# A fused linear-attention and mixer kernel: batch 1's front divided anew between VectorE and ScalarE, and its steps placed anew among batch 0's matmuls

## The chip, the cores and the metric

The kernel runs on one core of a Trainium2 chip. Its time is device microseconds (us) of that core, as the median of several executions. TensorE (PE) multiplies into PSUM, VectorE (DVE) and ScalarE (ACT) move and change data and empty PSUM, GpSimd (POOL) and SyncE (SP) issue transfers, and all engines work through instruction queues of their own in order, held together by semaphores.

## The reference

There are 8 batches, 8 heads, 576 rows and 64 columns per head. Linear attention gives x, and a mixer works on it, first across rows (tokens) and then across channels.

```python
def phi(x): return np.where(x > 0, x, np.exp(x) - 1.0) + 1.0
q_p, k_p = phi(q), phi(k)
kv  = np.einsum('bhsd,bhse->bhde', k_p, v);  z = np.sum(k_p, axis=2)
num = np.einsum('bhsd,bhde->bhse', q_p, kv)
den = np.einsum('bhsd,bhd->bhs', q_p, z)[..., None] + 1e-06
x = (num / den)                               # as (8, 576, 512)
h = np.maximum(x.transpose(0, 2, 1) @ w_tok1, 0.0) @ w_tok2      # 576 -> 256 -> 576
u = x + h.transpose(0, 2, 1)
out = u + np.maximum(u @ w_ch1, 0.0) @ w_ch2                     # 512 -> 1536 -> 512
```

## The kernel before, in words

Rows are laid out as 9 slots of 64. A batch has four full tiles of 128 rows (`r` = 0 to 3) and one half tile (`r = R = 4`, 64 rows). The half tiles of the two batches of a pair are put together in one tile `ut` and are taken through the channel mixer once for both.

The steps of a batch, by the names that the change and the prediction use:

- `phi_exp`, `phi_add`, `phi_end` (L125, L131, L139 and L140): phi of half of q's or k's heads, as exp on ScalarE, then x + 1, a minimum and a maximum on VectorE. `vcast` (L151) casts v.
- `qtr` (L180, copied by L187): q transposed by PE, in batch 1 only; later batches do it with a DMA (`qtr_dma`).
- `kv` (L169): k^T v for all heads, with a column of ones for z, then two copies to `kvbd` (L175).
- `nd` (L210, then L219, L221, L222): numerator and denominator of x for two row tiles and half the heads (`g`), six times a batch. VectorE adds the epsilon, takes the reciprocal and multiplies.
- `mm1` (L248, ReLU on ScalarE L251), `mm2` (L261): the token mixer's two matmuls. `mm2` leaves u = x + h. Batch 1 has it as `mm2_half`, by halves of the columns (L297, L300): row tiles 0 and 1 add x by a matmul with the identity and are copied by ScalarE (L303), row tiles 2 and 3 are added by VectorE (L305). The last rows of batch 0 are made by `mm2_first_tail` (L458), those of batch 1 by `mm2(1, [R])`, those of later pairs by `mm2_tails` (L282, L286).
- `utr` (L316): u transposed by PE for batch 1, by pairs of column tiles; `utr_tail` (L481) transposes `ut`.
- `mm3` (L503, ReLU L510 or, on VectorE, L507), `mm3_tail` (L517), `mm4` (L529) and `mm4_end` (L546): the channel mixer, its sum with u and the transfer of the result.

The order is written out by hand. `run` takes a list of large steps (`big`: `mm3` and `mm4` of one batch) and a list of fillers with the number of the large step that each follows; these make the next batch's front. For batch 0, `m4_0(kc)` goes through `mm4` of all four row tiles with one piece of the contraction at a time, and its four accumulators (`held`) take all four banks of `ps_big`. The front of batch 1 therefore works in `ps_sm`, a pool of two buffers of two PSUM banks each, taken in turn: a step that wants a buffer waits till the one two places before it has been emptied. After the last `m4_0` came, in a row, output sums, `mm2_half`, `utr` and `mm2(1, [R])`, and only then `mm3` of batch 1.

```python
    work = ctx.enter_context(tc.tile_pool(name="work", bufs=2))
    ps_big = ctx.enter_context(tc.tile_pool(name="ps_big", bufs=4, space=bass.MemoryType.PSUM))
    ps_sm = ctx.enter_context(tc.tile_pool(name="ps_sm", bufs=2, space=bass.MemoryType.PSUM))
```

The transfers of batch 1's k, q and v and of the second piece of `w_ch2` are gated on earlier transfers; batch 2's q waits for that second piece.

Of the kernel before, what the change touches and what calls it, by code (L numbers as in the profile page):

```python
# [9 lines left out]
FP32 = mybir.dt.float32  # L10
# [8 lines left out]
def kernel(  # L19
# [26 lines left out]
    R = 4  # L46
# [115 lines left out]
    def kv(n, cs):  # L162
        b = n % 2
        ps = ps_sm.tile([128, 2, 512], FP32, name="kv_ps", tag="sm")[:, :, 0:2 * D1].rearrange(
            "p a (c e) -> p a c e", c=2)
        for c in cs:
            for t in range(T):
                for a, i in QUARTERS:
                    nc.tensor.matmul(out=ps[half[i], a, c], lhsT=kp[half[a], c, t, i],  # L169
                                     rhs=vs[half[a], 2 * c + i, t],  # L170
                                     start=(t == 0), stop=(t == T - 1))
        cs = slice(cs[0], cs[-1] + 1)
        for i in range(2):
            at = slice(i * D1, (i + 1) * D1)
            nc.scalar.copy(out=kvbd[b][half[i], cs, :, at].transpose([0, 2, 1, 3]),  # L175
                           in_=ps[half[i], :, cs])

    def qtr_mm(c, ts, tp):
        for s_, t in enumerate(ts):
# [48 lines left out]
    def nd(n, g, rs):  # L228
        nd_mm(n, g, rs)
        nd_end(n, g, rs)  # L230

    ALL = slice(0, DM)
    COLS = [slice(0, DM // 2), slice(DM // 2, DM)]

# [7 lines left out]
    def mm1(n):  # L242
        b = n % 2
        ps = ps_sm.tile([128, NT, DM], FP32, name="a_ps", tag="sm")
        for mt in range(NT):
            ms = slice(128 * mt, 128 * mt + 128)
            for r in range(R1):
                nc.tensor.matmul(out=ps[:, mt], lhsT=w1t[:, b, ms] if r == R else w1[:, r, ms],  # L248
                                 rhs=x[b][:, r, :], start=(r == 0), stop=(r == R))
        for mt in range(NT):  # L250
            nc.scalar.activation(out=ar[b][:, mt, :], in_=ps[:, mt], func=AF.Relu)  # L251

    def mm2(n, rs, add=False):

        b = n % 2
        m = len(rs)
        ps = bank().rearrange("p (a d) -> p a d", a=1) if n == 1 else ps_sm.tile(
            [128, 2, DM], FP32, name="h_ps", tag="sm")
        for i, r in enumerate(rs):
            for kt in range(NT):  # L260
                nc.tensor.matmul(out=ps[:, i], lhsT=w2v(kt, r, b),  # L261
# [2 lines left out]
            if add:  # L264
                nc.tensor.matmul(out=ps[:, i], lhsT=identity, rhs=x[b][:, r, :], start=False,
                                 stop=True)
        if rs[0] == R:
            h = half[b]
            nc.vector.tensor_tensor(out=ut[n // 2 % 2][h], in0=ps[h, 0], in1=x[b][h, R], op=ALU.add)
        elif add:  # L270
            nc.scalar.copy(out=u[b][:, rs[0]:rs[0] + m], in_=ps[:, 0:m])
        else:
            nc.vector.tensor_tensor(out=u[b][:, rs[0]:rs[0] + m], in0=ps[:, 0:m],  # L273
                                    in1=x[b][:, rs[0]:rs[0] + m], op=ALU.add)
# [10 lines left out]
            h = half[b]  # L285
            nc.vector.tensor_tensor(out=ut[p % 2][h], in0=ps[h], in1=x[b][h, R], op=ALU.add)  # L286

    def mm2_half(n, c):
        b = n % 2
        cs = COLS[c]  # L290
        for rs in ([0, 1], [2, 3]):
            ps = ps_sm.tile([128, 2, 512], FP32, name="h_ps", tag="sm")[:, 0].rearrange(
                "p (r c) -> p r c", r=2)
            add = rs[0] == 0
            for i, r in enumerate(rs):
                if add:
                    nc.tensor.matmul(out=ps[:, i], lhsT=identity, rhs=x[b][:, r, cs],  # L297
                                     start=True, stop=False)
                for kt in range(NT):
                    nc.tensor.matmul(out=ps[:, i], lhsT=w2v(kt, r), rhs=ar[b][:, kt, cs],  # L300
                                     start=(kt == 0 and not add), stop=(kt == NT - 1))
            if add:
                nc.scalar.copy(out=u[b][:, 0:2, cs], in_=ps)  # L303
            else:
                nc.vector.tensor_tensor(out=u[b][:, 2:4, cs], in0=ps, in1=x[b][:, 2:4, cs],  # L305
                                        op=ALU.add)

    def utr(n, js):
        b = n % 2
        for jp in js:  # L310
            tp = ps_sm.tile([128, 2, 8, 128], BF16, name="tp", tag="sm")[:, 0].rearrange(
                "p (j r) c -> p j r c", j=2)
            for i in range(2):
                j = 2 * jp + i
                for r in range(R):
                    nc.tensor.transpose(out=tp[:, i, r, :],  # L316
                                        in_=u[b][:, r, 128 * j:128 * j + 128], identity=identity)
            dst = uT[b][:, :, 2 * jp:2 * jp + 2].transpose([0, 2, 1, 3])
            if jp == 0:
                nc.vector.tensor_copy(out=dst, in_=tp)  # L320
            else:
                nc.scalar.copy(out=dst, in_=tp)

# [119 lines left out]
    def mm2_first(c, rs):  # L445
        cs = COLS[c]
        ps = bank().rearrange("p (r c) -> p r c", r=2)
        for i, r in enumerate(rs):
            for kt in range(NT):
# [1 line left out]
                                 start=(kt == 0), stop=(kt == NT - 1))  # L451
        nc.vector.tensor_tensor(out=u[0][:, rs[0]:rs[0] + 2, cs], in0=ps,
                                in1=x[0][:, rs[0]:rs[0] + 2, cs], op=ALU.add)

    def mm2_first_tail():
        ps = sm_tile()[:, 0]
        for kt in range(NT):
            nc.tensor.matmul(out=ps[half[0]], lhsT=w2p[:, D * (T * kt + 2 * R):][:, 0:D],  # L458
                             rhs=ar[0][:, kt],
                             start=(kt == 0), stop=(kt == NT - 1))  # L460
        nc.vector.tensor_tensor(out=ut[0][half[0]], in0=ps[half[0]], in1=x[0][half[0], R],
                                op=ALU.add)

    def utr_first(js, put):
        tp = ps_sm.tile([128, 2, 8, 128], BF16, name="tp", tag="sm")[:, 0].rearrange(
# [234 lines left out]
    def steps(n):  # L700

        out_ = [("kv", lambda: kv(n, range(2)))]
        if n == 1:
            puts = [nc.scalar.copy, nc.vector.tensor_copy if n == 1 else nc.scalar.copy]
            out_ += [(f"qt{c}", lambda c=c: qtr(n, c, puts[c])) for c in range(2)]
        for i, rs in enumerate(([0, 1], [2, 3], [4])):
            for g in range(2):
                out_.append((f"nd{i}{g}", lambda g=g, rs=rs: nd(n, g, rs)))
        out_.append(("mm1", lambda: mm1(n)))
        if n > 1:  # L710
            out_ += [("mm2a", lambda: mm2(n, [0, 1])), ("mm2b", lambda: mm2(n, [2, 3]))]
            if n % 2:
                out_.append(("mm2t", lambda: mm2_tails(n // 2)))
            out_ += [("uta", lambda: utr_dma(n, [0, 1])), ("utb", lambda: utr_dma(n, [2, 3]))]
            if n % 2:
                out_.append(("utt", lambda: utr_tail_dma(n // 2)))
        return out_

    def run(bigs, fill):
        for i, big in enumerate(bigs):  # L720
            big()
            for s, fn in fill:
                if s == i:
                    fn()
        for s, fn in fill:
            assert s < len(bigs)

    m3 = lambda n, k0=0: [lambda mc=mc: mm3(n, mc) for mc in range(k0, NCH)]
    m3t = [lambda i=i: mm3_tail(i) for i in range(3)]
# [1 line left out]
                        for t in ts for i in range(3)]  # L731


    def m4_0(kc):
        for t in range(R):
            mm4(0, t, [kc], wait=True)

    big = [lambda mc=mc: mm3(0, mc, range(2, 4)) for mc in range(3)] + \
        [lambda mc=mc: mm3(0, mc, dve=mc in (3, 6, 9)) for mc in range(3, NCH)] + \
        [lambda kc=kc: m4_0(kc) for kc in range(NCH)]  # L740
    at0 = {"qt0": 12, "qt1": 14, "vc": 13, "kv": 14, "nd00": 15, "nd01": 16, "nd10": 17,
           "nd11": 18, "nd20": 19, "nd21": 20, "mm1": 21}
    fill = [(2, mm2_first_tail)]
    for ex, ad, en, nm, c in ((2, 2, 3, "k", 0), (5, 5, 6, "k", 1), (8, 8, 9, "q", 0),
                              (11, 11, 12, "q", 1)):
        fill += [(ex, lambda nm=nm, c=c: phi_exp(nm, 1, 2 * c, 2)),
                 (ad, lambda nm=nm, c=c: phi_add(nm, 1, 2 * c, 2)),
                 (en, lambda nm=nm, c=c: phi_end(nm, 1, 2 * c, 2))]
    late = [("vc", lambda: vcast(1, 0)), ("vc", lambda: vcast(1, 1, nc.vector.tensor_copy))]
    fill += [(21, lambda g=g: phi("q", 2, g)) for g in range(2)]  # L750
    fill += [(22, lambda: qtr_dma(2)), (22, lambda: load_all(3, "qkv"))]
    first = steps(1)
    for nm, fn in first[1:2] + late + first[2:3] + first[0:1] + first[3:]:
        fill += [(at0[nm], fn)]
    fill += [(23, fn) for fn in (
        lambda: mm4_end(0, 0), lambda: mm4_end(0, 1), lambda: mm2_half(1, 0),
        lambda: mm4_end(0, 2), lambda: mm2_half(1, 1), lambda: utr(1, [0]),
        lambda: mm2(1, [R]), lambda: utr(1, [1]), lambda: mm4_end(0, 3))]
    run(big, sorted(fill, key=lambda e: e[0]))


    for mc in range(3):
        mm3(1, mc, range(0, 2))
    utr_tail(0)
    big = [lambda mc=mc: mm3(1, mc, range(2, 4)) for mc in range(3)] + [lambda mc=mc: mm3(1, mc, dve=mc in (5, 8)) for mc in range(3, NCH)] + m3t + m4(0, [4, 5, 6, 7, 8])
    at1 = {"kv": 8, "nd00": 10, "nd01": 11, "nd10": 12, "nd11": 13, "nd20": 14, "nd21": 15,
           "mm1": 17, "mm2a": 18, "mm2b": 19, "mm2t": 21, "uta": 18, "utb": 19}
    fill = [(s, lambda g=g: phi("k", 2, g)) for g, s in ((0, 0), (1, 2))]
    fill += [(4, lambda: vcast(2, 0)), (5, lambda: vcast(2, 1, nc.vector.tensor_copy))]
    fill += [(at1[nm], fn) for nm, fn in steps(2)]  # L770
# [59 lines left out]
```

## Time and profile before

| what | value |
|---|---|
| median of 3 runs | 263.5 us (263.29 to 263.62) |
| profiled execution | 263.5 us, of which the span is 261.7 us |
| PE, VectorE, ScalarE, POOL busy | 252.9, 158.6, 130.8, 35.7 us |
| granted TensorE clock | 1.000 |
| batch 1's front, `nd` to the first `mm3` of batch 1 | 38.9 to 53.5 us |

The span runs from the first to the last instruction. An operation's row gives line, engine, operation, what it writes and reads, shape and count. Matmuls are pipelined, so one is shown longer than the time till the next one starts.

### The profile page before, as it was taken

How to read it: one execution, taken by the hardware profiler on the slowest of the kernel's cores; microseconds unless marked ns; L12 is line 12 of the kernel's file. 1: busy time of each engine (PE TensorE's matmuls, PEld its weight loads, DVE VectorE, ACT ScalarE, POOL GpSimd, SP SyncE). 2: the span in 40 equal slices, each digit the busy share in tenths (PEclk: the TensorE clock that was granted, in tenths of full speed). 3: DMA queues.
4: the chain of work that ended last, by engine and by line, in shares of the span. 5: the costliest groups of instructions: out<-in, count | busy, mean ns of one | idle time of the engine just before them, and what ended most of it. 6: DMA issues, size and time to landing. Idle time of an engine off the chain costs nothing.

```text
span 261.7 us, 5138 instructions
## 1 busy us (share of the span) xinstructions
PE 252.9 (97%) x2102; PEld 132.5 (51%) x2102; DVE 158.6 (61%) x313; ACT 130.8 (50%) x202; POOL 35.7 (14%) x58
## 2 busy tenths in 40 slices
PE   7699999999999999999999999999999999999994
PEld 3484455554744554455554554455564554444642
DVE  5765969966739686948674377939674263420122
ACT  4664873378374468336780468235780453026300
POOL 9760220110001300030001300030001300000000
PEclk9999999999999999999999999999999999999999
DMA  7999999899407994799999970860075500730043
GB/s 251 256 204 273 382 187 364 251 189 379 181 8 141 203 369 196 153 234 380 407 313 212 361 297 1 172 161 21 3 143 109 123 3 2 154 105 0 3 102 98
DMA packets 50087, 48.34 MB, mean 185 GB/s; under 512 B 30288, under 2 KB 35536, under 8 KB 50064
## 3 DMA queue, kind: packets, MB, share of 16 engines
q1 hardware_dynamic: 41904, 35.53, 46.1%
q0 software_dynamic: 7440, 11.44, 21.0%
q10 hardware_dynamic: 720, 1.05, 1.2%
q8 instruction: 16, 0.26, 0.4%
q14 instruction: 7, 0.06, 0.1%
HBM read 35.85 MB, written 9.44 MB: 173 GB/s over the span
## 4 chain that ended last, share of the span: by engine, by line
PE 91%; DMA 3%; ACT 2%; POOL 1%; issue 1%; DVE 1%; ACTq 0%; POOLq 0%
PE h_ps L529 33%; PE c_ps L503 32%; PE a_ps L248 6%; PE c_ps L517 4%; PE h_ps L261 4%; PE nd_ps L210 3%; DMA cr<-in_v_dram 3%; PE kv_ps L169 2%; PE h_ps L566 1%; PE bank L440 1%; POOL qT L610 1%; PE bank L378 1%; PE h_ps L282 1%; PE bank L405 1%; ACT u L303 0%
## 5 line engine op out<-in xcount | busy, mean ns | idle before, releaser
L503 PE MATMUL c_ps<-uT,wc 128*128 128x512 bf16 x384 | 91.5, 379 | 0.0
L510 ACT ACTIVATE cr<-c_ps 128x512 bf16<-128x512 f32 x91 | 53.4, 599 | 75.6 <-PE c_ps L503 75.4
L529 PE MATMUL h_ps<-wc,cr 128*128 128x512 bf16 x372 | 84.9, 379 | 0.0
L529 PEld LDWEIGHTS <-cr 128*128 128x128 bf16 x372 | 35.7, 98 | 41.6 <-issue 1.2
L503 PEld LDWEIGHTS <-wc 128*128 128x128 bf16 x384 | 35.8, 98 | 36.6 <-issue 1.2
L551 POOL DMA_DIRECT2D out_dram<-o_sb x24 | 14.5, 606 | 150.8 <-DVE o_sb L546 150.6
L546 DVE TENSOR_TENSOR o_sb<-h_ps,u 128x512 f32<-128x512 f32 x31 | 21.0, 687 | 21.0 <-PE h_ps L529 21.0
L222 DVE TENSOR_TENSOR x<-nd_ps,den 128x512 bf16<-128x512 f32 (+1 forms) x42 | 25.3, 602 | 1.5
L139 DVE TENSOR_SCALAR e<-e 128x1152 bf16<-128x1152 bf16 x30 | 14.0, 468 | 15.6 <-ACT e L125 15.5
L125 ACT ACTIVATE e<-q_raw 128x1152 bf16<-128x1152 f32 x16 | 18.5, 1160 | 6.2 <-DMA q_raw<-in_q_dram 6.2
L273 DVE TENSOR_TENSOR u<-h_ps,x 128x1024 bf16<-128x1024 f32 x12 | 14.3, 1218 | 10.1 <-PE h_ps L261 10.1
L125 ACT ACTIVATE e<-k_raw 128x1152 bf16<-128x1152 f32 x16 | 18.7, 1169 | 2.4 <-DMA k_raw<-in_k_dram 2.3
L219 DVE TENSOR_SCALAR den<-nd_ps 128x8 f32<-128x8 f32 (+1 forms) x42 | 6.8, 163 | 17.9 <-PE nd_ps L210 17.2
L210 PEld LDWEIGHTS <-qT 128*128 128x128 bf16 x140 | 11.4, 98 | 9.3 <-issue 0.2
L210 PE MATMUL nd_ps<-kvbd,qT 128*128 128x130 bf16 x140 | 15.1, 223 | 0.0
L248 PE MATMUL a_ps<-x,w 128*128 128x512 bf16 x56 | 14.4, 379 | 0.0
L556 DVE TENSOR_TENSOR o_sb<-h_ps,ut 128x512 f32<-128x512 f32 x4 | 2.8, 689 | 18.7 <-PE h_ps L529 18.7
L151 ACT CAST vs<-v_raw 128x1152 bf16<-128x1152 f32 x12 | 13.9, 1160 | 0.0
L251 ACT ACTIVATE ar<-a_ps 128x512 bf16<-128x512 f32 x14 | 7.6, 595 | 11.0 <-PE a_ps L248 11.0
L261 PE MATMUL h_ps<-ar,w2p 128*128 128x512 bf16 x48 | 12.5, 379 | 0.1
L140 DVE TENSOR_TENSOR qp<-e,y 128x1152 bf16<-128x1152 bf16 x16 | 12.1, 758 | 0.6
L131 DVE TENSOR_SCALAR y<-q_raw 128x1152 bf16<-128x1152 f32 x16 | 12.1, 757 | 0.3
(111 smaller groups left out, 221.7 us busy)
## 6 DMA issues: line engine op xcount, KB each, us to landing
k_raw<-in_k_dram SPq DMA_DIRECT2D x16, 576.0 KB, 9.4
q_raw<-in_q_dram SPq DMA_DIRECT2D x16, 576.0 KB, 7.7
v_raw<-in_v_dram SPq DMA_DIRECT2D x14, 576.0 KB, 11.1
out_dram<-o_sb POOLq DMA_DIRECT2D x24, 256.0 KB, 4.7
wc<-in_moe_w_ch_dram POOLq DMA_DIRECT2D x8, 384.0 KB, 9.7
out_dram<-o_sb SPq DMA_DIRECT2D x9, 128.0 KB, 2.3
out_dram<-o_sb ACTq DMA_DIRECT2D x7, 128.0 KB, 2.6
out_dram<-o_sb POOLq DMA_DIRECT2D x6, 128.0 KB, 5.4
```

The costliest lines, as they stand in the source:

```text
L125: nc.scalar.activation(out=e, in_=f, func=AF.Exp)
L139: nc.vector.tensor_scalar(out=e, in0=e, scalar1=1.0, scalar2=None, op0=ALU.min)
L210: nc.tensor.matmul(out=o[:, a], lhsT=qT[b][:, t0:t0 + 128], rhs=kvbd[b][:, c, a], start=True, stop=True)
L222: nc.vector.tensor_tensor(out=x[b][:, rs[0]:rs[0] + m, HG * D * g:HG * D * (g + 1)].rearrange("p r (h d) -> p r h d", h=HG), in0=v_[:, :, ...
L248: nc.tensor.matmul(out=ps[:, mt], lhsT=w1t[:, b, ms] if r == R else w1[:, r, ms], rhs=x[b][:, r, :], start=(r == 0), stop=(r == R))
L261: nc.tensor.matmul(out=ps[:, i], lhsT=w2v(kt, r, b), rhs=ar[b][:, kt, :], start=(kt == 0), stop=(kt == NT - 1 and not add))
L273: nc.vector.tensor_tensor(out=u[b][:, rs[0]:rs[0] + m], in0=ps[:, 0:m], in1=x[b][:, rs[0]:rs[0] + m], op=ALU.add)
L503: nc.tensor.matmul(out=ps, lhsT=wc1[:, kj, 128 * mc:128 * mc + 128], rhs=uT[b][:, :, kj], start=(kj == 0), stop=(kj == NDM - 1))
L510: nc.scalar.activation(out=cr[b][:, mc, :], in_=ps, func=AF.Relu)
L529: nc.tensor.matmul(out=ps, lhsT=crt[:, kc, :] if t == 8 else cr[b][:, kc, 128 * r:128 * r + 128], rhs=wc2[:, kc, :], start=(kc == 0), stop ...
L546: nc.vector.tensor_tensor(out=o, in0=ps, in1=u[b][:, r, :], op=ALU.add)
L551: (nc.scalar if last and e else put).dma_start(out=outv[2 * p + b, :, 2 * r0 + e:2 * r0 + e + 2 * m - 1:2], in_=live["o"][half[e], 0:m])
```

## The change

Batch 1's front is built from other pieces and placed elsewhere.

- `nd_two` takes the place of `nd` for batch 1. VectorE scales two of four heads and ScalarE the other two, as activations of 64 columns with the reciprocal as scale. The half tile of both halves of the heads is one such step, so there are five in place of six.
- The second of the two copies to `kvbd`, and the ReLU of the second half of `mm1`, go to VectorE in batch 1.
- `mm1` stands at 19.5 in place of 21. `mm2` goes by full rows (`mm2_half` is gone), and `utr` transposes two row tiles at a time, both copied by ScalarE. Both stand among the `m4_0` steps and no longer behind them.
- `m4_0` is divided: by two row tiles for each piece of the contraction, and by single row tiles for the last two pieces.
- `mm2_first_tail` and `mm2(1, [R])` are replaced by `mm2_tails(0)`, which takes the last rows of batches 0 and 1 together.
- phi of batch 2's q, its transposing transfer and the loads of batch 3 stand at 19.5 and 20.5 in place of 21 and 22.

```diff
@@ kv
-            nc.scalar.copy(out=kvbd[b][half[i], cs, :, at].transpose([0, 2, 1, 3]),
-                           in_=ps[half[i], :, cs])
+            copy = nc.vector.tensor_copy if n == 1 and i else nc.scalar.copy
+            copy(out=kvbd[b][half[i], cs, :, at].transpose([0, 2, 1, 3]), in_=ps[half[i], :, cs])
@@ new
+    def nd_two(rs, gs):
+        b = 1
+        ps = ps_sm.tile([128, 2, 512], FP32, name="nd_ps", tag="sm")
+        at = [(r, g) for r in rs for g in gs]
+        for s_, (r, g) in enumerate(at):
+            o = ps[:, s_, 0:4 * D1].rearrange("p (i a e) -> p a i e", i=2, a=2)
+            for a in range(2):
+                t0 = D * (T * (2 * a + g) + 2 * r - (b if r == R else 0))
+                nc.tensor.matmul(out=o[:, a], lhsT=qT[b][:, t0:t0 + 128], rhs=kvbd[b][:, g, a],
+                                 start=True, stop=True)
+        v_ = ps[:, :, 0:HG * D1].rearrange("p s (h e) -> p s h e", h=HG)
+        den = work.tile([128, 2, HG], FP32, name="den", tag="den")
+        nc.vector.tensor_scalar(out=den, in0=v_[:, :, :, D:D1].rearrange("p s h o -> p s (h o)"),
+                                scalar1=EPS, scalar2=None, op0=ALU.add)
+        nc.vector.reciprocal(out=den, in_=den)
+        xs = x[b].rearrange("p r (g h d) -> p r g h d", g=2, h=HG)
+        dst = xs[:, R] if len(gs) == 2 else xs[:, rs[0]:rs[0] + 2, gs[0]]
+        nc.vector.tensor_tensor(out=dst[:, :, 0:2], in0=v_[:, :, 0:2, 0:D],
+                                in1=den[:, :, 0:2, None].to_broadcast([128, 2, 2, D]), op=ALU.mult)
+        for s_, (r, g) in enumerate(at):
+            for h in range(2, HG):
+                nc.scalar.activation(out=xs[:, r, g, h], in_=v_[:, s_, h, 0:D], func=AF.Copy,
+                                     scale=den[:, s_, h:h + 1])
@@ mm1
-            nc.scalar.activation(out=ar[b][:, mt, :], in_=ps[:, mt], func=AF.Relu)
+            if n == 1 and mt:
+                nc.vector.tensor_scalar(out=ar[b][:, mt, :], in0=ps[:, mt], scalar1=0.0,
+                                        scalar2=None, op0=ALU.max)
+            else:
+                nc.scalar.activation(out=ar[b][:, mt, :], in_=ps[:, mt], func=AF.Relu)
@@ utr
+    def utr(n, rs):
+        b = n % 2
+        tp = ps_sm.tile([128, 2, 8, 128], BF16, name="tp", tag="sm")[:, 0].rearrange(
+            "p (r j) c -> p r j c", r=2)
+        for i, r in enumerate(rs):
+            for j in range(NDM):
+                nc.tensor.transpose(out=tp[:, i, j, :],
+                                    in_=u[b][:, r, 128 * j:128 * j + 128], identity=identity)
+        nc.scalar.copy(out=uT[b][:, rs[0]:rs[0] + 2], in_=tp)
@@ the order
-        [lambda kc=kc: m4_0(kc) for kc in range(NCH)]
-    at0 = {"qt0": 12, "qt1": 14, "vc": 13, "kv": 14, "nd00": 15, "nd01": 16, "nd10": 17,
-           "nd11": 18, "nd20": 19, "nd21": 20, "mm1": 21}
-    fill = [(2, mm2_first_tail)]
...
-    fill += [(23, fn) for fn in (
-        lambda: mm4_end(0, 0), lambda: mm4_end(0, 1), lambda: mm2_half(1, 0),
-        lambda: mm4_end(0, 2), lambda: mm2_half(1, 1), lambda: utr(1, [0]),
-        lambda: mm2(1, [R]), lambda: utr(1, [1]), lambda: mm4_end(0, 3))]
+    at = list(range(NCH))
+    for kc in range(NCH - 2):
+        for h in range(2):
+            big.append(lambda kc=kc, h=h: m4_0([kc], [2 * h, 2 * h + 1]))
+            at.append(NCH + kc + h / 2)
+    for t in range(R):
+        big.append(lambda t=t: m4_0([NCH - 2, NCH - 1], [t]))
+        at.append(2 * NCH - 2 + t)
...
+    fill += [(12.5, lambda: qtr(1, 0)), (13.5, lambda: vcast(1, 0)),
+             (13.5, lambda: vcast(1, 1, nc.vector.tensor_copy)),
+             (14.5, lambda: qtr(1, 1, nc.vector.tensor_copy)), (14.5, lambda: kv(1, range(2))),
+             (15.5, lambda: nd_two([0, 1], [0])), (15.5, lambda: nd_two([0, 1], [1])),
+             (17, lambda: nd_two([2, 3], [0])), (18, lambda: nd_two([2, 3], [1])),
+             (18.5, lambda: nd_two([R], [0, 1])), (19.5, lambda: phi("q", 2, 0)),
+             (19.5, lambda: mm1(1)), (19.5, lambda: phi("q", 2, 1)),
+             (20.5, lambda: mm2(1, [0, 1], add=True)), (20.5, lambda: mm2(1, [2, 3])),
+             (20.5, lambda: qtr_dma(2)), (20.5, lambda: load_all(3, "qkv")),
+             (21.5, lambda: mm2_tails(0)), (21.5, lambda: utr(1, [0, 1])),
+             (22, lambda: mm4_end(0, 0)), (22, lambda: utr(1, [2, 3])),
+             (23, lambda: mm4_end(0, 1)), (24, lambda: utr_tail(0)), (24, lambda: mm4_end(0, 2)),
+             (25, lambda: mm4_end(0, 3))]
+    run(big, fill, at)
```

The three first `mm3` of batch 1, which stood in two parts around `utr_tail(0)`, are whole again and follow it.

More of the change, by code (lines that the diff above doesn't have):

```diff
@@ L256, in mm2 @@
         m = len(rs)
-        ps = bank().rearrange("p (a d) -> p a d", a=1) if n == 1 else ps_sm.tile(
-            [128, 2, DM], FP32, name="h_ps", tag="sm")
+        ps = ps_sm.tile([128, 2, DM], FP32, name="h_ps", tag="sm")
         for i, r in enumerate(rs):
@@ L266, in mm2 @@
                                  stop=True)
[L267 to L270, printed above, removed]
+        if add:
             nc.scalar.copy(out=u[b][:, rs[0]:rs[0] + m], in_=ps[:, 0:m])
@@ L286, in mm2_tails @@
             nc.vector.tensor_tensor(out=ut[p % 2][h], in0=ps[h], in1=x[b][h, R], op=ALU.add)
-    def mm2_half(n, c):
+    def utr(n, rs):
         b = n % 2
[L290 to L322, printed above, removed]
+        tp = ps_sm.tile([128, 2, 8, 128], BF16, name="tp", tag="sm")[:, 0].rearrange(
[5 more added lines that the diff above has]
+        nc.scalar.copy(out=uT[b][:, rs[0]:rs[0] + 2], in_=tp)
     COLS = [slice(0, DM // 2), slice(DM // 2, DM)]
@@ L453, in mm2_first @@
                                 in1=x[0][:, rs[0]:rs[0] + 2, cs], op=ALU.add)
[L455 to L462, printed above, removed]
     def utr_first(js, put):
@@ L702, in steps @@
         out_ = [("kv", lambda: kv(n, range(2)))]
-        if n == 1:
-            puts = [nc.scalar.copy, nc.vector.tensor_copy if n == 1 else nc.scalar.copy]
-            out_ += [(f"qt{c}", lambda c=c: qtr(n, c, puts[c])) for c in range(2)]
         for i, rs in enumerate(([0, 1], [2, 3], [4])):
@@ L709, in steps, with run @@
         out_.append(("mm1", lambda: mm1(n)))
[L710 to L716, printed above, removed]
-        return out_
-    def run(bigs, fill):
-        for i, big in enumerate(bigs):
+        out_ += [("mm2a", lambda: mm2(n, [0, 1])), ("mm2b", lambda: mm2(n, [2, 3]))]
+        if n % 2:
+            out_.append(("mm2t", lambda: mm2_tails(n // 2)))
+        out_ += [("uta", lambda: utr_dma(n, [0, 1])), ("utb", lambda: utr_dma(n, [2, 3]))]
+        if n % 2:
+            out_.append(("utt", lambda: utr_tail_dma(n // 2)))
+        return out_
+    def run(bigs, fill, at=None):
+        at = range(len(bigs)) if at is None else at
+        for i, big in zip(at, bigs):
             big()
@@ L725, in run @@
         for s, fn in fill:
-            assert s < len(bigs)
+            assert s in at
     m3 = lambda n, k0=0: [lambda mc=mc: mm3(n, mc) for mc in range(k0, NCH)]
@@ L731, with m4_0 @@
                         for t in ts for i in range(3)]
-    def m4_0(kc):
-        for t in range(R):
-            mm4(0, t, [kc], wait=True)
+    def m4_0(kcs, ts):
+        for t in ts:
+            mm4(0, t, kcs, wait=True)
     big = [lambda mc=mc: mm3(0, mc, range(2, 4)) for mc in range(3)] + \
-        [lambda mc=mc: mm3(0, mc, dve=mc in (3, 6, 9)) for mc in range(3, NCH)] + \
-        [lambda kc=kc: m4_0(kc) for kc in range(NCH)]
-    at0 = {"qt0": 12, "qt1": 14, "vc": 13, "kv": 14, "nd00": 15, "nd01": 16, "nd10": 17,
-           "nd11": 18, "nd20": 19, "nd21": 20, "mm1": 21}
-    fill = [(2, mm2_first_tail)]
+        [lambda mc=mc: mm3(0, mc, dve=mc in (3, 6, 9)) for mc in range(3, NCH)]
+    at = list(range(NCH))
[6 more added lines that the diff above has]
+        at.append(2 * NCH - 2 + t)
+    fill = []
     for ex, ad, en, nm, c in ((2, 2, 3, "k", 0), (5, 5, 6, "k", 1), (8, 8, 9, "q", 0),
-                              (11, 11, 12, "q", 1)):
+                              (11, 11, 12.5, "q", 1)):
         fill += [(ex, lambda nm=nm, c=c: phi_exp(nm, 1, 2 * c, 2)),
@@ L748 @@
                  (en, lambda nm=nm, c=c: phi_end(nm, 1, 2 * c, 2))]
[L749 to L754, printed above, removed]
-    fill += [(23, fn) for fn in (
-        lambda: mm4_end(0, 0), lambda: mm4_end(0, 1), lambda: mm2_half(1, 0),
-        lambda: mm4_end(0, 2), lambda: mm2_half(1, 1), lambda: utr(1, [0]),
-        lambda: mm2(1, [R]), lambda: utr(1, [1]), lambda: mm4_end(0, 3))]
@@ L759 @@
[L759 to L765, printed above, removed]
+    fill += [(12.5, lambda: qtr(1, 0)), (13.5, lambda: vcast(1, 0)),
[11 more added lines that the diff above has]
+             (25, lambda: mm4_end(0, 3))]
@@ L766 @@
+    run(big, fill, at)
+    big = [lambda mc=mc: mm3(1, mc, dve=mc in (5, 8)) for mc in range(NCH)] + m3t + \
+        m4(0, [4, 5, 6, 7, 8])
     at1 = {"kv": 8, "nd00": 10, "nd01": 11, "nd10": 12, "nd11": 13, "nd20": 14, "nd21": 15,
-           "mm1": 17, "mm2a": 18, "mm2b": 19, "mm2t": 21, "uta": 18, "utb": 19}
+           "mm1": 17, "mm2a": 18, "mm2b": 19, "uta": 18, "utb": 19}
     fill = [(s, lambda g=g: phi("k", 2, g)) for g, s in ((0, 0), (1, 2))]
```

## The prediction, made before the changed kernel ran

> **What bounds the kernel now.** I read the page first, then the chain of waits, then PE's order of time with the start of each matmul, and last the rows of the operations that the change adds.
>
> ```profile
> PE 252.9 (97%) x2102; PEld 132.5 (51%) x2102; DVE 158.6 (61%) x313; ACT 130.8 (50%) x202; POOL 35.7 (14%) x58
> PEclk9999999999999999999999999999999999999999
> ```
>
> PE is busy for 97% of the span and its clock is granted in full in every slice. Busy time says little here, since a 128x512 matmul is shown 379 ns long while the next one starts 0.216 us later. So I count steps from start to start (0.216 for 512 columns, 0.056 for a transpose). Whatever they exceed is a stall. From 25 us on PE hardly stalls: time is won or lost only by matmuls removed and by stalls that come or go.
>
> ```profile
> 33.93 1.16 ACT e L125
> 35.09 1.10 ACT qT L187 x2
> 36.18 1.06 ACT vs L151
> ...
> 50.03 0.59 ACT u L303
> ...
> 51.52 0.59 ACT u L303
> ```
>
> That is the chain of waits in batch 1's front, the stretch that the change rewrites. Here the end hangs on ScalarE twice: before `kv` and in `mm2_half`. PE's order of time shows the same places:
>
> ```profile
> 24.91 0.62 PE L458 MATMUL bank<-ar,w2p 128*64 128x512 bf16 x2
> 33.24 1.22 PE L529 MATMUL h_ps<-wc,cr 128*128 128x512 bf16 x4
> 38.94 0.40 PE L210 MATMUL nd_ps<-kvbd,qT 128*128 128x130 bf16 x4
> 50.67 0.27 PE L297 MATMUL h_ps<-x,identity 128*128 128x256 bf16 x1 [0.23 <-ACT u L303]
> 52.16 0.61 PE L316 MATMUL tp<-identity,u 128*128 128x128 bf16 x8 [0.24 <-ACT u L303]
> 57.65 4.20 PE L503 MATMUL c_ps<-uT,wc 128*128 128x512 bf16 x18
> ```
>
> The brackets show 0.23 and 0.24 idle. By starts each is a stall of 0.40 (last start before the first is 50.16, one step 0.11). At 53.42 there is 0.07 more. The 18 matmuls of the last line should take 17 x 0.216 + 0.38 = 4.05 us, so 0.15 is a stall (the ReLU of an earlier bank was late on a backed-up ScalarE).
>
> Four rows for what is added, from ScalarE's and VectorE's order of time (start, length, operation):
>
> ```profile
> 16.56 1.29 DVE L420 TENSOR_TENSOR x<-bank,den 128x512 bf16<-128x512 f32 x2 [0.44 <-PE bank L405]
> 16.68 0.93 ACT L429 ACTIVATE x<-bank,den 128x64 bf16<-128x64 f32 x4 [0.83 <-PE bank L405]
> 38.13 0.76 ACT L175 CAST kvbd<-kv_ps 64x260 bf16<-64x260 f32 x2 [0.89 <-PE kv_ps L169]
> 106.58 1.39 DVE L286 TENSOR_TENSOR ut<-h_ps,x 64x512 bf16<-64x512 f32 x2 [0.32 <-PE h_ps L282]
> ```
>
> **What it takes away.** Two 512-column matmuls of `mm2(1, [R])`: 0.43. `mm2_first_tail` (24.91 to 25.46, 0.55, and 0.09 ahead of it) becomes `mm2_tails(0)`, which costs the same elsewhere (L282 of batch 3: 105.91 to 106.47, and 0.09 ahead). `mm2` by full rows and `utr` by rows hold the same matmul time as before (20 x 0.109 against 10 x 0.216; 16 transposes each), so they cost nothing by themselves. The four stalls 0.40, 0.40, 0.07 and 0.15 go, as `mm2` now has matmuls of batch 0 behind it and ScalarE enters `mm3(1)` without a backlog. Sum: 0.43 + 1.02 = 1.45 us off.
>
> **The head moves only 0.50.** PE comes to the q transposes (34.30) 0.64 sooner, but `qp` comes from VectorE, whose row of work hangs on the second half of batch 1's k. That transfer was issued at 18.39 and took 10.2 us, so it lands at 28.6, and VectorE read it at 28.77. VectorE's chain can thus come 0.11 sooner: `qp` ends at 33.74 instead of 33.85, the transposes start at 33.80 instead of 34.30, and the two `qT` copies, the cast of `vs` and `kv` follow 0.50 sooner. Of the 0.64 removed, 0.14 (I take 0.15) stays as a stall.
>
> **`kvbd` by two engines: +0.05.** As built, VectorE's copy waits for ScalarE's, so they run in a row: 0.37 + 0.03 + VectorE's, against 0.76 for the pair now. Trace of before has no such VectorE row. Its bounds are 0.37 (ScalarE's own) and 0.68 (its 128x512 ReLU). I take 0.40, nearest to its 128x256 product of 0.42.
>
> **`nd_two`, the main term.** "At once" isn't what the built program says: ScalarE's first scaling waits for VectorE's product, not for the reciprocal alone. Count from a group's first matmul: the fourth ends at 0.40, VectorE starts 0.04 later and needs 0.17 + 0.20 + 0.42 with two handovers of 0.03 (`nd00` now: 38.94 to 39.81, where the product starts), so its half is done at 1.30. ScalarE's four take 0.03 + 0.93 and end at 2.26. With 0.05 to PE the buffer is back at 2.31 us; now it is back at 1.62 (product of 0.69). `ps_sm` has two buffers, so each group waits for the one two places before it. Let the first group start at 0, the second at 0.24. The third is due after six matmuls, at 1.77, and waits till 2.31: stall 0.54. The fourth is due at 3.41, and the second's buffer is back at 3.14: none. The fifth is due at 4.08; the third's comes at 4.62: 0.54. `mm1` is due at 5.72, just when the fourth's comes. Its fifth matmul reads the last rows of x, due at 6.58, there at 4.62 + 2.31 = 6.93: 0.35. Sum 1.43. VectorE's third `den` waits for ScalarE's first group as well, which is done by then.
>
> [...] Row first: a piece of 64 elements steps 0.205 (0.93 for four), a piece of 512 steps 0.49 (L510 at 30.85, the next at 31.34), so eight times the work costs 2.4 times the time. [...] The rows above show L420 and L429 side by side, but on two tiles; no row of before has two engines on one tile. [...]
>
> **`mm1` and its ReLU: +0.58.** ScalarE's queue holds the last scalings (till 6.88), exp of batch 2's q (1.16, till about 7.93), then the first half's ReLU. VectorE must finish that q (minimum 0.47, maximum 0.76, to 9.23) before the second half's ReLU, which it ends at 9.83. PE has issued `mm1` by 8.22 and four matmuls by 9.09; the second matmul of `mm2` is due at 9.30 and starts at 9.88. The exp waits for its transfer: issued 36.91, 6.6 us, landed 43.5, well before it is wanted at 45.3.
>
> **The two buffers again: +0.68.** `mm2` ends at 11.82, `mm2_tails` begins at 12.77. In batch 3 its two additions ended 2.06 after its first matmul (105.91 to 107.97), so its buffer is back at 14.89 with the handover. `utr(1, [2, 3])` is due at 14.21. ScalarE's copies of u and `uT` (about 1.0 each, L322) are covered: the first by 0.5 us, the second by 0.25 us of matmuls ahead of `mm3(1)`; if that cover went, the shortfall would be added.
>
> `qtr_dma(2)` and the loads of batch 3 leave SP's queue about 1 us later in step with VectorE. Batch 3's q is first read at 19 steps into the next stage, some 10 us after it lands: nothing. `mm4_end(0, 0)` stands behind the two `ut` additions on VectorE and gives its bank back at about 15.5, due at 16.85; output transfers on POOL's queue have nobody waiting: nothing. Other batches have the same order as now: nothing.
>
> **Sum:** -1.45 + 0.15 + 0.05 + 1.43 + 0.58 + 0.68 = +1.44 us. The profiled run took 263.5 us, span 261.7, which is also the median of the three. Forecast: 263.5 + 1.4 = 264.9 us.
>
> **Range.** The least sure size is four scalings. Four of ScalarE's smallest rows (64x2, 0.16) would be 0.64, each of three stalls 0.29 shorter: 264.1. Four without overlap (0.31 each) would be 1.26: 265.9. The `kvbd` copy's bounds, -0.03 and +0.28, lie within. Range 264.1 to 265.9.
>
> **Rivals.** (a) Scaling is at once after all, or the wait costs nothing: ScalarE starts 0.46 sooner, and the stalls of 0.54, 0.54 and 0.35 become 0.08, 0.08 and 0: 263.6, no change. For it: L420 and L429 overlap; against it: the wait in the built program. (b) Faster: PE's own queue covers every handover. Place: the two buffers of `ps_sm` and the ReLU. Price: 1.43 + 0.58 + 0.68 gone, 262.2. It decides where each handover is met by the time PE is due, so where a buffer of `nd_two` is back within 1.77 us and the ReLU and `ut` are 0.6 and 0.7 us sooner than counted. For it: the 0.43 to 0.86 us of matmuls of `m4_0` put between the steps; against it: the rows add up to 2.31. (c) Slower still: batch 2's q lands late and stands in ScalarE's queue ahead of the ReLU. It has 1.8 us to spare; 3 us late gives 266.1. Against it: its gate, the second piece of `wc2`, isn't moved.
>
> **Chances.** Forecast 0.82, (c) 0.05, (a) 0.08, (b) 0.05. A difference under 0.2% (0.5 us) can't be told from none. So faster 0.05, same 0.08, slower 0.87.
>
> **What would show it.** Right: PE waits in `nd_ps` and `a_ps` on ScalarE's x, near 0.5, 0.5 and 0.3; in `h_ps` on VectorE's `ar`, near 0.6; in `tp` on VectorE's `ut`, near 0.7; no wait on `u` of ScalarE. Wrong: ScalarE's scalings beginning beside VectorE's product, or `mm3(1)` starting before 54 us.

## The result, and the profile after

| | median | runs | profiled execution, its span |
|---|---|---|---|
| before | 263.56 us (263.29 to 263.73) | 4 | 263.5 us, 261.7 us |
| changed | 265.22 us (264.70 to 265.64) | 4 | 265.13 us, 263.3 us |

The changed kernel is slower: ratio 1.0063, 95% interval 1.0043 to 1.0083. That is 1.66 us by the medians; the forecast was 264.9 us.

The page of the changed kernel, in the lines that were shown of before:

```profile
PE 253.7 (96%) x2092; PEld 131.4 (50%) x2092; DVE 157.6 (60%) x310; ACT 135.2 (51%) x220; POOL 36.1 (14%) x58
PEclk9999999999999999999999999999999999999999
```

PE's share of busy time falls by one point and the clock is granted in full as before (1.000 in both). The page alone says no more than that PE now waits somewhere. The chain of waits says where (start, length, what):

```profile
39.73 0.94 ACT x L255 x4
...
42.17 0.94 ACT x L255 x4
...
44.62 0.93 ACT x L255 x4
45.55 1.06 ACT e L125
...
47.12 0.63 DVE qp L140
...
47.80 0.69 DVE ar L278
...
52.10 0.68 DVE ut L312
52.80 0.71 DVE ut L312
```

Before, the end hung on ScalarE's `u` twice. That is gone, and from `nd` on the chain now leaves PE for VectorE and ScalarE four times: for the scalings of three groups, the third time with batch 2's q and the ReLU in the same stretch, and for the two additions of the last rows. PE's order of time has five stalls there (the third scaling and the ReLU are one each), and one more at the q transposes:

```profile
33.60 0.68 PE L180 MATMUL tp<-identity,qp 128*128 128x128 bf16 x9 [0.17 <-DVE qp L140]
...
40.71 0.40 PE L242 MATMUL nd_ps<-kvbd,qT 128*128 128x130 bf16 x4 [0.45 <-ACT x L255]
...
43.15 0.40 PE L242 MATMUL nd_ps<-kvbd,qT 128*128 128x130 bf16 x4 [0.52 <-ACT x L255]
...
45.60 0.38 PE L274 MATMUL a_ps<-x,w1t 128*128 128x512 bf16 x1 [0.32 <-ACT x L255]
...
48.54 0.38 PE L290 MATMUL h_ps<-ar,w2p 128*128 128x512 bf16 x1 [0.41 <-DVE ar L278]
...
53.54 0.61 PE L320 MATMUL tp<-identity,u 128*128 128x128 bf16 x8 [0.50 <-DVE ut L312]
...
55.51 5.34 PE L494 MATMUL c_ps<-uT,wc 128*128 128x512 bf16 x24
```

A bracket counts from the modelled end of the matmul before it, so it is smaller than the stall. By starts the six are 0.33, 0.61, 0.68, 0.49, 0.57 and 0.67 us. The last line shows what was won: 24 matmuls at 23 x 0.216 + 0.38 = 5.35, so these first 24 of `mm3` of batch 1 have no stall.

The rows of what was added, from VectorE's and ScalarE's order of time:

```profile
37.85 0.43 DVE L176 CAST kvbd<-kv_ps 64x260 bf16<-64x260 f32 x1 [0.48 <-ACT kvbd L176]
...
41.65 0.42 DVE L251 TENSOR_TENSOR x<-nd_ps,den 128x256 bf16<-128x256 f32 x1
...
42.17 0.93 ACT L255 ACTIVATE x<-nd_ps,den 128x64 bf16<-128x64 f32 x4 [0.69 <-DVE x L251]
...
47.80 0.68 DVE L278 TENSOR_SCALAR ar<-a_ps 128x512 bf16<-128x512 f32 x1
```

ScalarE's four scalings do not begin beside VectorE's product but after it: 41.65 + 0.42 = 42.07, and ScalarE starts at 42.17.

The start-up up to the first `mm3` (21.04 to 21.60 us in nine of the profiles, 22.91 in one) and the wait at the q transposes behind it (none to 0.52) differ from profile to profile, whatever the kernel. The one with 22.91 is e3's, whose profiled execution took 265.12 us, 1.0 above its median. In e6 and e7 PE also waited behind `kv` for a transfer of `wc` (brackets of 0.28 and 0.26). Below I therefore compare stalls from start to start, times by ratio, and in places the stretch from the first `mm3` to the end of the span: 240.1 us before, 242.1 in the changed kernel, 242.3 in its repeat e8.

### The profile page after: what moved, and what is told of

Its sections match the earlier page's. It is cut to its first block, busy times and chain, and to the rows that moved or that the text cites. A ratio compares the mean times of both kernels' runs of the same rounds, so it can differ in the third digit from the quotient of the medians.

```text
span 263.3 us, 5140 instructions
## 1 busy us (share of the span) xinstructions
PE 253.7 (96%) x2092; PEld 131.4 (50%) x2092; DVE 157.6 (60%) x310; ACT 135.2 (51%) x220; POOL 36.1 (14%) x58
## 4 chain that ended last, share of the span: by engine, by line
PE 80%; DMA 7%; DVE 4%; POOL 3%; ACT 3%; issue 1%; SPq 0%; ACTq 0%; DVEq 0%; POOLq 0%
PE h_ps L520 31%; PE c_ps L494 28%; PE a_ps L274 5%; PE h_ps L290 5%; PE c_ps L508 4%; DMA k_raw<-in_k_dram 4%; DMA wc<-in_moe_w_ch_dram 4%; PE nd_ps L210 3%; PE kv_ps L169 2%; ACT x L255 1%; PE h_ps L557 1%; PE h_ps L308 1%; POOL qT L601 1%; POOL cr L117 1%; DVE y L131 1%
## 5 line engine op out<-in xcount | busy, mean ns | idle before, releaser
L222 DVE TENSOR_TENSOR x<-nd_ps,den 128x512 bf16<-128x512 f32 (+1 forms) x36 | 21.7, 603 | 1.2
L299 DVE TENSOR_TENSOR u<-h_ps,x 128x1024 bf16<-128x1024 f32 x13 | 15.5, 1219 | 10.5 <-PE h_ps L290 10.5
L219 DVE TENSOR_SCALAR den<-nd_ps 128x8 f32<-128x8 f32 (+1 forms) x36 | 5.9, 164 | 16.5 <-PE nd_ps L210 15.9
L290 PE MATMUL h_ps<-ar,w2p 128*128 128x512 bf16 x56 | 14.9, 379 | 0.5 <-DVE ar L278 0.4
L210 PEld LDWEIGHTS <-qT 128*128 128x128 bf16 x120 | 9.7, 98 | 7.8
L210 PE MATMUL nd_ps<-kvbd,qT 128*128 128x130 bf16 x120 | 13.0, 223 | 0.0
L131 DVE TENSOR_SCALAR y<-k_raw 128x1152 bf16<-128x1152 f32 x14 | 10.6, 756 | 3.0 <-DMA k_raw<-in_k_dram 2.8
```

Of the source, the lines that this page charges most:

```text
L131: nc.vector.tensor_scalar(out=y, in0=f, scalar1=1.0, scalar2=None, op0=ALU.add)
L210: nc.tensor.matmul(out=o[:, a], lhsT=qT[b][:, t0:t0 + 128], rhs=kvbd[b][:, c, a], start=True, stop=True)
L222: nc.vector.tensor_tensor(out=x[b][:, rs[0]:rs[0] + m, HG * D * g:HG * D * (g + 1)].rearrange("p r (h d) -> p r h d", h=HG), in0=v_[:, :, ...
L290: nc.tensor.matmul(out=ps[:, i], lhsT=w2v(kt, r, b), rhs=ar[b][:, kt, :], start=(kt == 0), stop=(kt == NT - 1 and not add))
```

## The experiments

The theory: the front is slower because three handovers through two PSUM buffers come late. They are the scalings of `nd_two`, done by two engines in turn; the ReLU behind batch 2's q; and the `ut` additions of `mm2_tails`. The rival in each run: that handover is covered or costs little, and the time goes into the new order as a whole, so that taking the handover away brings little.

### e1: VectorE scales all four heads

```diff
-        nc.vector.tensor_tensor(out=dst[:, :, 0:2], in0=v_[:, :, 0:2, 0:D],
-                                in1=den[:, :, 0:2, None].to_broadcast([128, 2, 2, D]), op=ALU.mult)
-        for s_, (r, g) in enumerate(at):
-            for h in range(2, HG):
-                nc.scalar.activation(out=xs[:, r, g, h], in_=v_[:, s_, h, 0:D], func=AF.Copy,
-                                     scale=den[:, s_, h:h + 1])
+        nc.vector.tensor_tensor(out=dst, in0=v_[:, :, :, 0:D],
+                                in1=den[:, :, :, None].to_broadcast([128, 2, HG, D]), op=ALU.mult)
```

> The changed kernel, but VectorE scales all four heads of each nd_two and ScalarE none. Theory (handovers): what the change loses is the time that a ps_sm buffer takes to come back. Without ScalarE's share it is back about 1.62 us after a group's first matmul, not 2.4, so the waits of 0.61, 0.68 and 0.49 in nd_ps and a_ps shrink to 0.3 in all, while the waits of mm2 on ar (0.5) and of utr on ut (0.6) stay: 263.7 us. Rival (load): VectorE then has 5 x 0.27 us more to do in the same stretch, and the wait only moves on to its ReLU or its additions: 265.0 to 265.4 us.

Measured: 263.93 us, ratio to before 1.0017 (1.0002 to 1.0031). Of the three stalls of the scaling the first is gone, and the others shrink to 0.16 and 0.10. The stalls on the ReLU and on `ut` stay (0.50 and 0.67), as PE's and VectorE's order of time shows:

```profile
47.61 0.38 PE L286 MATMUL h_ps<-ar,w2p 128*128 128x512 bf16 x1 [0.33 <-DVE ar L274]
...
52.62 0.61 PE L316 MATMUL tp<-identity,u 128*128 128x128 bf16 x8 [0.50 <-DVE ut L308]
...
46.87 0.69 DVE L274 TENSOR_SCALAR ar<-a_ps 128x512 bf16<-128x512 f32 x1 [0.34 <-ACT ar L277]
```

The stalls on the scaling fall from 1.78 to 0.26 us, and the ratio falls by 0.0046 (1.2 us; against the repeat e8, 1.5 us). So scaling by two engines costs most of the loss. The last line adds something: VectorE now had 0.34 us with nothing to do ahead of its ReLU and waited for ScalarE's ReLU of the other half. These two, on one tile, also go in turn.

### e2: `mm2_tails` behind `utr`, its transposing in the next stage

```diff
-             (21.5, lambda: mm2_tails(0)), (21.5, lambda: utr(1, [0, 1])),
+             (21.5, lambda: utr(1, [0, 1])),
...
-             (23, lambda: mm4_end(0, 1)), (24, lambda: utr_tail(0)), (24, lambda: mm4_end(0, 2)),
+             (23, lambda: mm4_end(0, 1)), (24, lambda: mm4_end(0, 2)), (24, lambda: mm2_tails(0)),
...
+    fill += [(3, lambda: utr_tail(0))]
```

> The changed kernel, but mm2_tails(0) stands behind both utr at step 24, and utr_tail(0) in the next stage at step 3. Theory (handovers): utr(1, [2, 3]) no longer waits for the two additions of ut, the 0.67 us in tp goes, nothing takes its place: 264.5 us. Rival (the end of the stage is bound elsewhere, by ScalarE's copies of uT): mm3 of batch 1 waits for uT instead, 265.2 us.

Measured: 264.68 us, ratio 1.0052 (1.0033 to 1.0072). The transposes no longer wait. Their row has no bracket, and no step before it exceeds its length:

```profile
51.92 0.61 PE L320 MATMUL tp<-identity,u 128*128 128x128 bf16 x8
```

The other four stalls stay at 0.61, 0.68, 0.48 and 0.57. The full rows and the division of `m4_0` are still there, and no stall stands at them; the place of `mm2_tails` cost its 0.67 us. The medians alone could not show this, as the ratio's interval overlaps that of the changed kernel. From the first `mm3` to the end the profile has 241.4 us, 0.7 to 0.9 less than the two of the changed kernel.

### e3: the split scaling kept, its steps farther apart

As e2, and in addition:

```diff
-             (15.5, lambda: nd_two([0, 1], [0])), (15.5, lambda: nd_two([0, 1], [1])),
+             (15.5, lambda: nd_two([0, 1], [0])), (16, lambda: nd_two([0, 1], [1])),
...
-             (18.5, lambda: nd_two([R], [0, 1])), (19.5, lambda: phi("q", 2, 0)),
-             (19.5, lambda: mm1(1)), (19.5, lambda: phi("q", 2, 1)),
-             (20.5, lambda: mm2(1, [0, 1], add=True)), (20.5, lambda: mm2(1, [2, 3])),
+             (19, lambda: nd_two([R], [0, 1])), (20, lambda: phi("q", 2, 0)),
+             (20, lambda: mm1(1)), (20, lambda: phi("q", 2, 1)),
+             (21.5, lambda: mm2(1, [0, 1], add=True)), (21.5, lambda: mm2(1, [2, 3])),
```

> The split between the two engines as in the changed kernel, but steps placed further apart: the second nd_two at 16, the last at 19, mm1 at 20, mm2 at 21.5, mm2_tails at 24, utr_tail in the next stage. Theory (handovers): the split's own waits stay (0.6, 0.3 and 0.5 in nd_ps and a_ps), those on ar and ut fall to 0.1 and 0.2: 263.9 us. Rival (load): no more than a few tenths from the changed kernel, 264.9 us or more.

Measured: 264.08 us, ratio 1.0032 (1.0018 to 1.0047).

```profile
42.05 0.40 PE L242 MATMUL nd_ps<-kvbd,qT 128*128 128x130 bf16 x4 [0.45 <-ACT x L255]
...
46.94 0.38 PE L274 MATMUL a_ps<-x,w1t 128*128 128x512 bf16 x1 [0.32 <-ACT x L255]
```

The wait on `ar` falls to 0.14. The transposes wait 0.17, now for VectorE's `u`, as `mm2_tails` stands behind them. The waits on the scaling keep 0.61, 0.25 and 0.48. More matmuls between the steps cover the ReLU and only a part of the scaling.

### e4: the divisions of work undone, in the order of e3

The order of e3, with the product of e1, and `kvbd`'s second copy and the second half's ReLU on ScalarE again. Full rows, `mm2_tails` and the divided `m4_0` stay.

```diff
-            copy = nc.vector.tensor_copy if n == 1 and i else nc.scalar.copy
+            copy = nc.scalar.copy
...
-            if n == 1 and mt:
+            if False:
```

> VectorE scales alone, kvbd and the ReLU of mm1 by ScalarE alone as before the change, steps placed as in the run with the wide placing; mm2 by full rows, utr by rows and mm2_tails(0) for both batches stay. Theory (handovers): of the waits after the q transposes only some 0.2 us on u is left, the 1.45 us that the change takes away are all that counts: 262.4 us, faster than both kernels. Rival (load): no better than before, 263.5 us.

Measured: 262.61 us, ratio 0.9962 (0.994 to 0.9983). It beats both kernels.

```profile
40.45 0.40 PE L242 MATMUL nd_ps<-kvbd,qT 128*128 128x130 bf16 x4
...
47.20 0.59 PE L286 MATMUL h_ps<-ar,w2p 128*128 128x512 bf16 x2
...
52.81 3.40 PE L490 MATMUL c_ps<-uT,wc 128*128 128x512 bf16 x15
```

No row of PE has a bracket between 37 and 57 us. The one stall left after `nd` begins is 0.17, at the second transposes of u (VectorE's `u`). `mm3` of batch 1 starts at 52.81, against 55.51 in the changed kernel and 53.55 before. So the places of e3 and the full rows are worth about 1 us. At these same places the three divisions of work between two engines take more than that away: the ratio is 1.0032 with them (e3) and 0.9962 without, 1.8 us. e4 undoes all three at once; e1 alone tells the scaling from the two others.

### e5: the split scaling alone, in the kernel before

```diff
+        k = 2 if n == 1 else HG
+        xs = x[b].rearrange("p r (g h d) -> p r g h d", g=2, h=HG)
         nc.vector.tensor_tensor(
-            out=x[b][:, rs[0]:rs[0] + m, HG * D * g:HG * D * (g + 1)].rearrange(
-                "p r (h d) -> p r h d", h=HG),
-            in0=v_[:, :, :, 0:D],
-            in1=den[:, :, :, None].to_broadcast([128, m, HG, D]), op=ALU.mult)
+            out=xs[:, rs[0]:rs[0] + m, g, 0:k], in0=v_[:, :, 0:k, 0:D],
+            in1=den[:, :, 0:k, None].to_broadcast([128, m, k, D]), op=ALU.mult)
+        for s_, r in enumerate(rs):
+            for h in range(k, HG):
+                nc.scalar.activation(out=xs[:, r, g, h], in_=v_[:, s_, h, 0:D], func=AF.Copy,
+                                     scale=den[:, s_, h:h + 1])
```

> The kernel before, with one part of the change alone: in batch 1's nd VectorE scales two heads of each group and ScalarE the other two, by activations of 64 columns; order, mm1, mm2 and transposes as before. Theory (handovers): a buffer comes back after 2.3 to 2.4 us instead of 1.62, the six nd start 1.10 us apart or less, so waits of 0.1 to 0.4 us appear in nd_ps from the third nd on, 0.6 in all, and ScalarE's later queue gives more: 264.2 to 264.7 us. Rival (the split is harmless, only the new order costs): 263.4 us, no waits in nd_ps.

Measured: 264.58 us, ratio 1.004 (1.001 to 1.0071), so 0.3 to 1.9 us slower than before by this part alone. Two groups wait 0.18 and 0.39. A third excess of 0.22 ahead of `mm1`'s last rows is a record that the trace lacks: four weight loads stand there and three matmuls. And a wait arose that nobody had expected, in PE's and VectorE's order of time:

```profile
52.41 0.60 PE L304 MATMUL h_ps<-ar,w2p 128*128 128x256 bf16 x4 [0.68 <-DVE u L309]
...
51.67 0.68 DVE L309 TENSOR_TENSOR u<-h_ps,x 128x512 bf16<-128x512 f32 x1
```

The scalings push batch 2's q back on ScalarE (its exp starts at 46.15, before at 43.60). VectorE, which finishes that q and then writes two output sums, reaches `u` at 51.67 (before at 50.47), and the last part of `mm2_half` waits 0.84 for its buffer; before, the transposes behind it had waited 0.40. The size came out as expected, the places only in part.

### e6: five buffers for `den`

VectorE's third and fifth `den` need not wait for ScalarE's scalings two groups before.

```diff
-        den = work.tile([128, 2, HG], FP32, name="den", tag="den")
+        den = work.tile([128, 2, HG], FP32, name="den5", tag="den5", bufs=5)
```

> The changed kernel with five buffers for nd_two's den in place of two, so that VectorE's first operation of the third to fifth group waits for PE alone and not also for ScalarE. Theory (handovers): that operation then starts 0.04 us after PE's last matmul instead of 0.11; the waits in nd_ps and a_ps on ScalarE fall from 0.61, 0.68, 0.49 to about 0.61, 0.61, 0.42, in all 0.14 us; the time is 265.1 us, too near to tell from the changed kernel. Rival (the late start has another cause, PE's last matmul or the den in use): starts stay 0.11 us late.

Measured: 265.32 us, ratio 1.0071 (1.0046 to 1.0095), so by time not to be told from the changed kernel (1.0063, 1.0074 in e8). The stalls can be told apart:

```profile
43.43 0.40 PE L242 MATMUL nd_ps<-kvbd,qT 128*128 128x130 bf16 x4 [0.45 <-ACT x L255]
...
45.80 0.38 PE L274 MATMUL a_ps<-x,w1t 128*128 128x512 bf16 x1 [0.25 <-ACT x L255]
```

In the changed kernel these two brackets were 0.52 and 0.32. By starts the three stalls on the scaling are 0.60, 0.61 and 0.41, against 0.61, 0.68 and 0.49. The wait for `den` had ended 0.45 us before PE's last matmul did (40.66 against 41.10 for the third `den` in the changed kernel's trace), and it still cost 0.07 us in each of the two groups whose stalls fell: see the last section.

### e7: ScalarE's four first, then VectorE's product

The same instructions as in the changed kernel; only the order in which the two are written is turned.

> The changed kernel with the two scalings of nd_two issued in the other order, ScalarE's four first and VectorE's product behind them. As built, ScalarE then waits for the reciprocal and the product waits for ScalarE's last. Theory (the two take one PSUM tile in turn, whichever comes first): ScalarE starts 0.1 us after the reciprocal, 0.4 sooner than now, but VectorE's product comes 0.03 us after ScalarE's last and holds up the next group's den on its queue; waits in nd_ps and a_ps double, 267 to 267.8 us. Rival (both could run at once, only the order of issue kept ScalarE back): the product runs beside ScalarE, waits shrink, 263.9 us.

Measured: 267.41 us, ratio 1.016 (1.0129 to 1.019). From PE's, VectorE's and ScalarE's order of time:

```profile
44.66 0.41 PE L242 MATMUL nd_ps<-kvbd,qT 128*128 128x130 bf16 x4 [0.95 <-DVE x L255]
...
42.38 0.42 DVE L255 TENSOR_TENSOR x<-nd_ps,den 128x256 bf16<-128x256 f32 x1 [1.06 <-ACT x L253]
...
43.21 0.93 ACT L253 ACTIVATE x<-nd_ps,den 128x64 bf16<-128x64 f32 x4 [0.86 <-DVE den L248]
```

Now VectorE stands still for 1.06 us while ScalarE scales, and as its next `den` is queued behind the product, every group is late (stalls of 0.61, 0.68, 1.11, 0.68, 0.91). So the two go in the order in which they are written, whichever it is. Rival (a) of the prediction, scaling at once, is out for the program as built.

### e8: the changed kernel again

> The changed kernel again, on the chip of the other runs, as their measure: 265.2 us, with waits of 0.61, 0.68, 0.49, 0.57 and 0.67 us in nd_ps, a_ps, h_ps and tp within 0.03. Theory (the rest of its spread lies ahead of the change): the start of the last transposes of batch 0 differs from profile to profile by some tenths, as the first transfers land.

Measured: 265.47 us, ratio 1.0074 (1.0054 to 1.0095). Stalls 0.61, 0.68, 0.48, 0.57 and 0.67: the same to 0.01 us. What differs lies ahead of them: 0.51 in place of 0.33 at the q transposes, and 0.10 in place of 0.15 ahead of the first `nd`.

## Why the prediction was right

Sign and places came out, and the size nearly. By its own terms (us, stalls from start to start in the changed kernel's profile):

| term | sum | measured |
|---|---|---|
| two matmuls of `mm2(1, [R])` gone | -0.43 | -0.43 (by their length; they are not in PE's order) |
| four stalls gone | -1.02 | -1.02 (none is left) |
| q transposes | +0.15 | +0.33 |
| `kvbd` copies in a row | +0.05 | +0.08 (0.148 ahead of `nd`, 0.065 before) |
| scaling through two buffers | +1.43 | +1.78 (0.609 + 0.681 + 0.485) |
| `mm2` on VectorE's ReLU | +0.58 | +0.57 |
| transposes on the `ut` additions | +0.68 | +0.67 |
| sum | +1.44 | +1.98 |

The sum of measured terms is 0.5 above the forecast, while the spans differ by only 1.6 (263.3 - 261.7). What lies between is the start-up: in this profile the first `mm3` started 0.37 us sooner than in that of before, and from there to the end the kernels differ by 1.97. So it is in part luck that the median came within about 0.3 us of the forecast. The repeat e8, on other executions, puts the difference at 1.95 us by ratio, near the sum of the measured terms.

**The places were right because the waits were read from the built program.** Three engines' rows laid end to end for each buffer gave three of the five stalls to 0.07 us or better: `ar`, `ut` and the first group. e1 took most of the scaling's waits away, e2 that on `ut`, e3 most of that on `ar` and that on `ut`, e4 all of them, and the time followed, in e2 by the profile only. Rival (b), that PE's queue covers the handovers, is out by the five stalls. Rival (c), that batch 2's q comes late, is out too: its exp starts at 45.42, right behind the last scaling, and its row shows no wait for a transfer.

**The mis-sized term is the scaling, 1.78 in place of 1.43.** Two sizes failed: "VectorE starts 0.04 later" and, of "ScalarE's four take 0.03 + 0.93", the 0.03. The two handovers of 0.03 inside VectorE's row were right. The buffer came back after 2.38 us in the first group (38.33 to 40.71) and 2.44 in the later ones (40.71 to 43.15), not 2.31. VectorE's product to ScalarE's first scaling took 0.095, not 0.03, in four groups. From the third group on, PE's last matmul to VectorE's `den` took 0.109, not 0.04. With 2.38 and 2.44 put in, the same count gives 0.61, 0.67 and 0.48.

**The q transposes: 0.33 in place of 0.15.** "PE comes 0.64 sooner" was counted from the start of PE in the profile of before. The transfer of k's second half that VectorE waits for landed 0.2 sooner (28.4 against 28.6), PE's start-up came 0.37 sooner. The term is a race between a transfer and PE. Of the eight profiles that have these steps at the same places up to there, seven had 0.22 to 0.52 and e3's, where PE started late, had none, so it had no single value to predict.

**The `kvbd` copy** took 0.43, not 0.40: it was sized by the product of a like width.

**The size of four scalings.** The trace has 0.93 for four, as the rows of before had. One scaling starts 0.20 to 0.21 after the other, but the last takes 0.32 from start to end, and only then is the buffer free: the first group's last ends at 40.66, and PE starts on the buffer at 40.71. The range's lower half rested on smaller pieces (0.16 each, by the 64x2 rows) that didn't come.

**Two engines on one tile.** In e7 and in the changed kernel the two engines take it in turn, by waits in the built program. What the chip would do without these waits no run here shows. Nor was a split of `nd` over two PSUM tiles tried; at that time the accumulators of `m4_0` hold all four buffers of `ps_big`.

## What to carry to other kernels

Before dividing the emptying of one PSUM tile between two engines, look in the built program whether the second waits for the first: if so the buffer can come back later, not sooner. Here it came back after 2.38 to 2.44 us where the rows of before give 1.62, and with two buffers PE paid for it at the third group, at the fifth and in `mm1` (0.61, 0.68 and 0.49 us). A step that gets matmuls of other work behind it is worth what it was hoped for only where these cover the whole way back of its buffer: in e3 they left 0.14 of the 0.57 us on the ReLU, but 0.61, 0.25 and 0.48 on the scaling. Lay the rows of that way end to end and compare with the due time two places on. Here new places (those of e3, not the change's own) without the division of work made the better kernel, 0.4% faster than before.

## What the runs showed of the hardware

In the traces here some instructions that wait for two others have one of the two waits on a semaphore instruction ahead of them (in the cases of the last column 0.017 us long on ScalarE, 0.021 on VectorE). Where that one ends last, the time from the end of the releasing instruction to the start of the waiting one is longer in the trace of the changed kernel:

| handover | ended by the instruction's own wait | ended by the wait ahead of it |
|---|---|---|
| PE to VectorE | 0.037 us (49 cases) | 0.109 us (3) |
| PE to ScalarE | 0.037 (83 of 91, the others 0.06) | 0.097 (14) |
| VectorE to ScalarE | no case with work of ScalarE's own; 0.032 to a transfer that it issues (8) | 0.095 (4) |

The trace of before has the last column too (13 cases of PE to ScalarE at 0.097, one of PE to VectorE at 0.108), so it could have been priced. e6 is the test for PE to VectorE: with the second wait of `den` gone, its three cases are at 0.037, and two stalls fell by 0.07 us each.

A matmul of 64 output rows after one of 128 came 0.093 us late, before (L458 at 24.91) and after (L308 at 51.43), and the first of 128 after it 0.095 late again; no row there shows a wait for another engine. The reason is not shown.
